# A partial sum scaled by VectorE first and copied by ScalarE, two early rows added up in another order, and narrow unread matmuls in two waits

## The chip, the cores and the metric

The kernel runs on one core of one Trainium2 chip. The metric is the device time of one execution in microseconds (us): the median of a few runs. For the kernel before it is 197.96 us (three runs, 197.57 to 198.35).

A core has five engines that matter here. TensorE (PE in the profile; PEld is its weight load) multiplies matrices into PSUM, an accumulation memory. VectorE (DVE), ScalarE (ACT) and GpSimd (POOL) do element work, and SyncE (SP) issues transfers. Each engine works off its own instruction list in order; between engines there are only waits on semaphores. Sixteen DMA engines move data between the chip's memory and the core.

## The reference

The computation has two steps. The first is a gated recurrence along 5056 tokens, for 4 batches and 256 channels:

```
f = lb + (1 - lb) * sigmoid(f_logit)
h[t] = f[t] * h[t-1] + (1 - f[t]) * x[t]
```

The second is a soft mixture of 8 experts with 4 slots each, on all 4 x 5056 = 20224 rows h:

```
logits = h @ phi                         # 32 slots
d = softmax of logits over all rows      # one column per slot
slot_in = d.T @ h                        # 32 x 256
slot_out[e] = relu(slot_in[e] @ w1[e]) @ w2[e]     # w1: 256 x 1024, w2: 1024 x 256
c = softmax of logits over the 32 slots  # one row per token
out = c @ slot_out                       # 20224 x 256, float32
```

No output row can be written before every row's logits are known and all experts are through: `slot_out` stands between the loads and the results.

## The kernel before

**Loads and recurrence.** The tokens of a batch are cut into groups of 512; a group of one batch is a "unit". For each unit SP loads `f_logit` and `x`, ACT takes the sigmoid, POOL multiplies, PE transposes to channels, DVE runs the recurrence as a scan (L313), and PE transposes back. PE forms the logits (L359), ACT their exponentials (L368), kept for all tokens in `etall` with 4 batches x 32 slots on the 128 partitions, and PE adds each group's part to `slot_ps` (L410). POOL issues the loads of the experts' weights (L137, L147), which turn float32 into bf16 on the way; the last weight is loaded in three pieces, into `w_t`.

**The drain.** After the last unit, PE closes the slot sums (L455). Two waits follow. In the first, DVE copies the sums out (`slot_sb`, L587) before PE can add up the batches (L591). In the second, DVE and ACT scale the result (`sin`, L602 and L603) before PE can start the experts (L621). In each of them PE works off `spin` (L150): six matmuls of 128 columns of weights on 256 columns of data, all of the first expert's weights, whose output nobody reads. A third `spin` of four stands at L724.

**The experts.** Experts 0 to 3 run side by side (L658) into `so4`. Experts 4 to 7 follow one after the other: for each, eight matmuls (L705), each with one eighth of the hidden units (`wide`) and of the weights. They add to `so_ps`, except for the last four of expert 7, which wait for the last pieces of its weights and go to `sb_ps`. `so_ps` also takes `so4` (L719). When `so_ps` is complete it is scaled by `rcs`, one over the sums of exponentials: `part_b` (bf16, ACT, L712) and `part` (float32, DVE, L713). When `sb_ps` is complete, DVE makes `slot_out` = `sb_ps` x `rcs` + `part` (L728).

**Two early rows.** Rows r = 0 and r = 1 of each run of 16 tokens, in batch 3's first 2048 tokens, don't wait for `slot_out`. PE has multiplied their exponentials with expert 7's hidden units ahead of time (`gs`, L680 and L682), so that four matmuls with the last four weight parts (`early_row`, L692) and one with `part_b` (`early_part`, L698) give each row directly, in `early_ps[r]`. ACT scales them (L734) and SP sends them off (L736).

**The order.** It is written out by hand: the program's order is each engine's order. PE runs two `sb_ps` matmuls, `early_row(0, 0, 2)`, both `early_part`, two `sb_ps` matmuls, `early_row(0, 2, 2)`, `early_row(1, 0, 4)`. The framework that places the waits lets two engines that read one PSUM tile do so one after the other, in program order.

**The results.** For each block of tokens PE multiplies `etall` with `slot_out` (L755) or with `slot_bd`, a form of it made by POOL for two batches at once (L738, L811). DVE (L745) and ACT (L749) divide by the row sums and write to SBUF, and SP sends it off. The first block goes off in five pieces (`pieces`, L774; SP issues at L785), the others in large blocks (`couple`, L804, SP at L817; `whole`, L793, SP at L802; `rest`, L819, SP at L834). SP's order is: both early rows, the five pieces, the blocks.

Of the kernel before, what the change touches and what calls it, by code (L numbers as in the profile page):

```python
# [13 lines left out]
ACT = mybir.ActivationFunctionType  # L14
# [4 lines left out]
def kernel(  # L19
# [10 lines left out]
    nc = tc.nc  # L30
    B, S, D = x.shape
    E = moe_w1.shape[0]
    F = moe_w1.shape[2]
    NS = moe_phi.shape[1]
# [97 lines left out]
    w1_sb = [wts.tile([P, DC, F], BF16, name=f"w1_sb{e}") for e in range(E)]  # L132
# [17 lines left out]
    def spin(dst, k, w):  # L150
        for _ in range(k):
            nc.tensor.matmul(dst[:, ds(0, w)], w1_sb[0][:, 0, :P], w1_sb[0][:, 0, :w],
                             start=True, stop=True, skip_group_check=True)

    W_AT = {9: 1, 17: 1, 25: 1, 31: 1, 32: 1, 33: 2, 34: 3, 36: 6}
    w_next = [0]
# [5 lines left out]
    with tc.tile_pool(name="sp2", bufs=3) as sp2, \  # L162
# [9 lines left out]
        slot_bank = pslot.tile([P, 2, D], F32, name="slot_ps")  # L172
# [215 lines left out]
        def row_sums(i):  # L388

            t0, n_r = blocks[i]  # L390
            ew = etall[:, ds(t0, P * n_r)].rearrange("s (p r) -> s p r", r=n_r)
            for r in range(n_r):
                nc.tensor.matmul(sums[:, ds((t0 // P + r) * B, P)], ew[:, :, r], ones,
                                 start=True, stop=True, skip_group_check=True)
            if i == len(blocks) - 1:
                nc.tensor.matmul(rs_ps[:, n_grp * R - 1, ds(0, B // 2)],
                                 left.rearrange("s t u -> s (t u)"), pair_ones,
                                 start=True, stop=True, skip_group_check=True)
# [53 lines left out]
        def late_slots():  # L452
            for r in range(R):
                for b in range(B):
                    nc.tensor.matmul(slot_ps[ds(b * NS, NS), :], ets[last][:, r, b],  # L455
                                     hts[last][:, b, r],
                                     start=False, stop=r == R - 1,
                                     skip_group_check=True)
# [20 lines left out]
        for n in range(n_unit):  # L479
# [14 lines left out]
            else:  # L494
# [40 lines left out]
                if n == n_unit - 2:  # L535
                    tail = psp.tile([P, 2, G], F32, name="tail", tag="sp")
# [44 lines left out]
        late_weights()  # L581
        slots(odd)
        late_slots()
        spin(tail[:, 1], 6, D)
        slot_sb = hpool.tile([P, G, DC], BF16, name="slot_sb", tag="h")
        slot_sb = slot_sb.rearrange("p t o -> p (t o)").bitcast(F32)[:, ds(0, D)]
        nc.vector.tensor_copy(slot_sb, slot_ps)  # L587
# [2 lines left out]
        for o in range(DC):  # L590
            nc.tensor.matmul(sin_ps[:, o], slot_v[:, o], rep[:, 0],  # L591
                             start=True, stop=True, skip_group_check=True)
        spin(slot_bank[:, 1], 6, D)

    with tc.tile_pool(name="ew", bufs=1) as ew, \
         tc.tile_pool(name="pm", bufs=2, space=PSUM) as pm, \
# [17 lines left out]
        for q in range(E // Q):  # L614
            hi = ew.tile([P, F], BF16, name=f"hi{q}")
            for k in range(2):
                hi_ps = (psu.tile([P, H], F32, name="hi_ps", tag="up") if q == 0 else
                         pbig.tile([P, H], F32, name="hi_ps", tag=f"hi_ps{k}"))
                for o in range(DC):
                    for j in range(Q):  # L620
                        nc.tensor.matmul(hi_ps[ds(j * NS, NS)], sin[:, o],  # L621
                                         w1_sb[q * Q + j][:, o, ds(k * H, H)],
                                         start=(o == 0), stop=(o == DC - 1),
                                         skip_group_check=True)
# [6 lines left out]
        rcs = ew.tile([P, 1], F32, name="rcs")  # L631
        for q in range(E // Q):
# [4 lines left out]
            if q == 0:  # L637
# [4 lines left out]
                dst = hid[:, :, :, ds(0, SPE)]  # L642
                dst = bass.AP(tensor=dst.tensor, offset=dst.offset,
                              ap=[list(dst.ap[0]), [Q * NS, FC], [NS + SPE, Q], [1, SPE]])
# [11 lines left out]
        for e in range(Q):  # L656
            for fc in range(FC):
                nc.tensor.matmul(so4_ps[ds(fc % 4 * NS, NS), :], hid[:, fc, e],  # L658
                                 w2_sb[e][:, fc],
                                 start=(e == 0 and fc < 4),  # L660
                                 stop=(e == Q - 1 and fc >= FC - 4),
                                 skip_group_check=True)
# [7 lines left out]
        n_late = FC // 2  # L670
        gs = ew.tile([P, n_late, 2, P], BF16, name="gs")
        hi_v = his[1].rearrange("p (c f) -> p f c", f=FC)
        so_ps = pm.tile([P, D], F32, name="so_ps", tag="pm")
# [3 lines left out]
        for i in range(0, n_late, 2):  # L677
            g_ps = psu.tile([P, 2, 2, P], F32, name="g_ps", tag="up")
            for k in range(2):
                nc.tensor.matmul(g_ps[:, k], hi_v[tail_b, FC - n_late + i + k], ex[tail_b],  # L680
                                 start=True, stop=True, skip_group_check=True)
            nc.scalar.copy(gs[:, ds(i, 2)].rearrange("p k r t -> p (k r t)"),  # L682
                           g_ps.rearrange("p k r t -> p (k r t)"))
        part = ew.tile([P, D], F32, name="part")
        part_b = ew.tile([P, D], BF16, name="part_b")
        e_only = ew.tile([P, 2, P], BF16, name="e_only")
# [3 lines left out]
        early_ps = [psu.tile([P, D], F32, name="early_ps", tag="up") for _ in range(2)]  # L690

        def early_row(r, k, n):  # L692
            for i in range(k, k + n):
                nc.tensor.matmul(early_ps[r], gs[:, i, r], w2_sb[E - 1][:, FC - n_late + i],
                                 start=r == 0 and i == 0, stop=i == n_late - 1,
                                 skip_group_check=True)

        def early_part(r):  # L698
            nc.tensor.matmul(early_ps[r], e_only[:, r], part_b, start=r == 1, stop=False,
                             skip_group_check=True)  # L700

        for j in range(Q):
            for fc in range(FC):
                late = j == Q - 1 and fc >= FC - n_late
                nc.tensor.matmul(sb_ps if late else so_ps,  # L705
                                 wide[:, fc, j].rearrange("p b s -> p (b s)"),
                                 w2_sb[Q + j][:, fc],
                                 start=(j == 0 and fc == 0) or (late and fc == FC - n_late),
                                 stop=j == Q - 1 and fc in (FC - n_late - 1, FC - 1),
                                 skip_group_check=True)  # L710
                if j == Q - 1 and fc == FC - n_late - 1:
                    nc.scalar.activation(part_b, so_ps, ACT.Copy, scale=rcs)  # L712
                    nc.vector.tensor_scalar_mul(part, so_ps, rcs)  # L713
                if j == Q - 1 and fc == FC - 3:
                    early_row(0, 0, 2)
                    early_part(0)
                    early_part(1)
            if j == 0:
                nc.tensor.matmul(so_ps, rep2, so4, start=False, stop=False,  # L719
                                 skip_group_check=True)  # L720
                row_sums(1)
            if j == 1:
                row_sums(2)
                spin(unread, 4, D)  # L724
                q = n_grp * R - 1
                nc.vector.reciprocal(rrow[:, wide_r:q], rs_ps[:, wide_r:q])
                nc.vector.reciprocal(rrow[:, q, ds(0, B // 2)], rs_ps[:, q, ds(0, B // 2)])
        nc.vector.scalar_tensor_tensor(slot_out, sb_ps, rcs, part, ALU.mult, ALU.add)  # L728
        early_row(0, 2, 2)
        early_row(1, 0, 4)  # L730
        early = ew.tile([P, 2, D], F32, name="early")
        to_b = out[ds((B - 1) * S, P * wide_r)].rearrange("(p r) d -> p r d", r=wide_r)
        for r in range(2):
            nc.scalar.activation(early[:, r], early_ps[r], ACT.Copy,  # L734
                                 scale=rrow[:, r, ds(B - 1, 1)])
# [140 lines left out]
```

## Time and profile before

| | |
|---|---|
| median of three runs | 197.96 us (197.57 to 198.35) |
| the profiled execution | 198.21 us |
| its span, first to last instruction | 196.4 us |
| PE busy | 149.9 us (76%), 1196 matmuls |
| DVE busy | 144.1 us (73%) |
| ACT busy | 142.6 us (73%) |
| POOL busy | 103.3 us (53%) |
| read from memory, written to it | 58.23 MB, 20.71 MB |
| chain that ended last | DMA 37%, PE 25%, DVE 13%, ACT 5%, POOL 4%, issue 4% |

No engine is busy all the time, and the chain changes hands often. A share of busy time is a mean over stages with different limits; it has to be read by stage. The profile's page cuts the span into 40 slices for that. The row PEclk there is the share of TensorE's full clock that was granted, in tenths. A chain entry "DMA x" is the time from a transfer's issue to its landing, and "issue" is time in which an engine waited for nothing that the profile shows. In a timeline, the bracket at the end of a line gives the idle time before an instruction and what ended it.

### The profile page before, as it was taken

The numbers are of one execution on the slowest core, as the hardware profiler recorded it, in microseconds if no ns is written. First come the engines' busy times: TensorE is split into PE (matmuls) and PEld (weight loads), VectorE is DVE, ScalarE is ACT, GpSimd is POOL, SyncE is SP. The second block draws the span as 40 slices with busy tenths as digits, with TensorE's granted clock in tenths as the row PEclk, the third lists the DMA queues.
The fourth block names the chain that finished last, engine by engine and source line by source line (L and its number), as shares of the span: only waits on it lengthen the run. The fifth ranks groups of instructions, "written<-read, shape, count | busy, mean of one in ns | idle before, by whom it ended". The sixth has DMA issues, their size and how long they took to land.

```text
span 196.4 us, 3258 instructions
## 1 busy us (share of the span) xinstructions
PE 149.9 (76%) x1196; PEld 105.8 (54%) x1196; DVE 144.1 (73%) x185; ACT 142.6 (73%) x201; POOL 103.3 (53%) x78
## 2 busy tenths in 40 slices
PE   0687579789979979897998888999889999920000
PEld 0475458577766858665776766668664434300000
DVE  2669789998799999999999999343277988920000
ACT  3688778899699998999998797334089999950000
POOL 2689586894988588894969976291030000000000
PEclk9999999996999999999999999999995555555555
DMA  6999999999999999999999999999749999999994
GB/s 205 420 422 418 430 430 420 427 425 333 405 427 424 398 343 422 427 417 308 405 419 385 259 222 214 214 214 213 138 162 432 422 432 424 427 427 437 444 444 173
DMA packets 14161, 70.75 MB, mean 360 GB/s; under 512 B 1585, under 2 KB 2866, under 8 KB 10178
## 3 DMA queue, kind: packets, MB, share of 16 engines
q1 hardware_dynamic: 11520, 62.13, 76.5%
q0 software_dynamic: 2624, 8.42, 21.5%
q8 instruction: 9, 0.15, 0.3%
q14 instruction: 6, 0.05, 0.1%
q10 hardware_dynamic: 2, 0.00, 0.0%
HBM read 58.23 MB, written 20.71 MB: 402 GB/s over the span
## 4 chain that ended last, share of the span: by engine, by line
DMA 37%; PE 25%; DVE 13%; ACT 5%; POOL 4%; issue 4%; ACTq 0%; SPq 0%; POOLq 0%
DMA x_t<-in_x_dram 14%; DVE h L313 10%; PE op L811 8%; DMA w_t<-in_moe_w_dram 8%; DMA f_t<-in_f_logit_dram 7%; DMA w_sb<-in_moe_w_dram 7%; POOL u_t L246 4%; PE hp L326 4%; ACT oc L749 3%; PE up L267 3%; DVE ht L345 3%; PE sp L261 2%; PE op L755 2%; PE lg L359 1%; PE slot_ps L183 1%
## 5 line engine op out<-in xcount | busy, mean ns | idle before, releaser
L246 POOL TENSOR_TENSOR u_t<-s_t,x_t 128x1024 bf16<-128x1024 bf16 (+1 forms) x39 | 82.5, 2131 | 21.8 <-ACT s_t L235 12.3
L313 DVE TENSOR_TENSOR_SCAN h<-a,h,up 128x512 bf16<-128x512 f32 (+1 forms) x72 | 86.9, 1253 | 3.9 <-PE up L267 2.6
L235 ACT ACTIVATE s_t<-f_t 128x2048 bf16<-128x2048 f32 (+2 forms) x23 | 38.4, 1669 | 7.1 <-DMA f_t<-in_f_logit_dram 7.1
L326 PE MATMUL hp<-ident_f,h 128*128 128x128 f32 (+1 forms) x160 | 29.4, 308 | 8.0 <-DVE ht L345 5.8
L326 PEld LDWEIGHTS hp<-ident_f,h 128*128 128x128 f32 (+1 forms) x160 | 23.4, 207 | 18.7 <-DVE ht L345 10.9
L261 PE MATMUL sp<-ident_f,s_t 128*128 128x128 f32 x144 | 21.3, 291 | 6.8 <-ACT s_t L235 4.5
L295 ACT ACTIVATE a<-sp,lbs 128x1024 f32<-128x1024 bf16 x24 | 25.5, 1117 | 0.6 <-PE sp L261 0.6
L749 ACT ACTIVATE oc<-op,rrow 128x256 f32<-128x256 f32 x62 | 24.5, 508 | 0.2
L811 PE MATMUL op<-slot_bd,etall 64*128 64x512 bf16 x62 | 23.6, 594 | 0.4 <-POOL slot_bd L738 0.3
L261 PEld LDWEIGHTS sp<-ident_f,s_t 128*128 128x128 f32 x144 | 17.4, 150 | 8.7 <-ACT s_t L235 5.0
L745 DVE TENSOR_TENSOR oc<-op,rrow 128x512 f32<-128x512 f32 x31 | 20.0, 685 | 2.0 <-PE op L811 1.9
L302 ACT ACTIVATE a<-sp,lbs 128x512 f32<-128x512 bf16 (+2 forms) x22 | 17.8, 857 | 3.8 <-PE sp L261 3.5
L267 PE MATMUL up<-ident_f,u_t 64*128 64x64 f32 x192 | 17.6, 229 | 2.4 <-POOL u_t L246 2.4
L183 PE MATMUL slot_ps<-rep,ident_f 128*128 128x256 f32 x52 | 17.0, 422 | 1.0 <-POOL rep L86 1.0
L267 PEld LDWEIGHTS up<-ident_f,u_t 64*128 64x128 f32 x192 | 13.9, 138 | 6.3 <-POOL u_t L246 2.8
L811 PEld LDWEIGHTS <-etall 64*128 64x128 bf16 x62 | 9.2, 155 | 13.5 <-issue 7.8
L345 DVE COPY ht<-hp 128x512 f32<-128x512 f32 (+1 forms) x20 | 13.4, 670 | 1.4 <-PE hp L326 1.4
L345 ACT COPY ht<-hp 128x512 f32<-128x512 f32 (+1 forms) x20 | 11.7, 583 | 3.5 <-PE hp L326 3.4
L313 DVE TENSOR_TENSOR_SCAN h<-a,up 128x512 bf16<-128x512 f32 x8 | 9.3, 1207 | 2.5 <-PE up L261 2.5
L183 PEld LDWEIGHTS slot_ps<-rep,ident_f 128*128 128x128 f32 x52 | 8.3, 193 | 3.0 <-POOL rep L86 1.2
L359 PE MATMUL lg<-h,phi 128*32 128x512 bf16 (+1 forms) x80 | 9.4, 389 | 0.3 <-ACT et L383 0.2
L261 PE MATMUL up<-ident_f,u_t 128*128 128x128 f32 x48 | 8.9, 314 | 0.5 <-POOL u_t L246 0.5
(126 smaller groups left out, 150.3 us busy)
## 6 DMA issues: line engine op xcount, KB each, us to landing
f_t<-in_f_logit_dram SPq DMA_DIRECT2D x12, 1024.0 KB, 13.3
x_t<-in_x_dram SPq DMA_DIRECT2D x12, 1024.0 KB, 12.0
out_dram<-oc SPq DMA_DIRECT2D x6, 2048.0 KB, 13.7
w_sb<-in_moe_w_dram POOLq DMA_DIRECT2D x14, 512.0 KB, 11.1
f_t<-in_f_logit_dram SPq DMA_DIRECT2D x12, 512.0 KB, 8.4
x_t<-in_x_dram SPq DMA_DIRECT2D x12, 512.0 KB, 9.9
out_dram<-oc SPq DMA_DIRECT2D x4, 896.0 KB, 6.3
out_dram<-ob SPq DMA_DIRECT2D x1, 2048.0 KB, 9.8
```

What stands on the lines that cost most here:

```text
L183: nc.tensor.matmul(slot_bank[:, 1], ident_f, wide_rep, start=False, stop=False, skip_group_check=True)
L235: nc.scalar.activation(s_t, f_t, ACT.Sigmoid, scale=-1.0)
L246: nc.gpsimd.tensor_tensor(uts[n][:, :r], s_t[:, :r], x_t[:, :r], ALU.mult)
L261: nc.tensor.transpose(ps[:, :, r], t[:, r], ident_f)
L267: nc.tensor.transpose(v[:, :, r], t(r)[k].bitcast(F32), ident_f[k, k])
L295: nc.scalar.activation(a, sp[:, :, :, :, o], ACT.Identity, scale=nomlb[:, ds(o, 1)], bias=1.0)
L313: nc.vector.tensor_tensor_scan(h[:, :T, o], decays[n // 2, o][:, n % 2, :T], up[:, :T, o], hs[number(g - 1, b)][:, ds(used(g - 1) - 1, 1), ...
L326: nc.tensor.transpose(hp[:n_p, r], hw[:, :n_p, r], ident_f)
L345: copy(hts[g][:n_p, b].rearrange("p r d -> p (r d)").bitcast(F32), hps.pop(n)[:n_p].rearrange("p r c -> p (r c)"))
L745: nc.vector.tensor_tensor(ob, op, scale.broadcast_to(list(ob.shape)), ALU.mult)
L749: nc.scalar.activation(ob[:, i], op[:, i], ACT.Copy, scale=scale[:, i])
L811: nc.tensor.matmul(op.rearrange("p u d -> p (u d)"), ew[:, :, r], slot_bd[ds(j * 2 * NS, 2 * NS)].rearrange("s u d -> s (u d)"), start=Tru ...
```

## The change

Three edits. The line numbers before L157 stay; later ones move by 6 or 7.

1. `part` comes first, from `so_ps`, by DVE; ACT then makes `part_b` as a plain copy of `part`.
2. The order of PE's matmuls for the two early rows: the first two of both rows stand ahead of the last two `sb_ps` matmuls, and `early_part` closes each row's sum.
3. In the two waits of the drain, `spin` goes from six matmuls to two, and 21 narrow ones follow: 32 columns of the same weights on the same 256 columns of data, with the output going round the four groups of 32 partitions.

```diff
+    def narrow(dst, k):
+        for i in range(k):
+            nc.tensor.matmul(dst[ds(i % B * NS, NS), ds(0, D)], w1_sb[0][:, 0, ds(0, NS)],
+                             w1_sb[0][:, 0, ds(0, D)], start=True, stop=True,
+                             skip_group_check=True)
...
-        spin(tail[:, 1], 6, D)
+        spin(tail[:, 1], 2, D)
+        narrow(tail[:, 1], 21)
...
-        spin(slot_bank[:, 1], 6, D)
+        spin(slot_bank[:, 1], 2, D)
+        narrow(slot_bank[:, 1], 21)
...
         def early_row(r, k, n):
             for i in range(k, k + n):
                 nc.tensor.matmul(early_ps[r], gs[:, i, r], w2_sb[E - 1][:, FC - n_late + i],
-                                 start=r == 0 and i == 0, stop=i == n_late - 1,
-                                 skip_group_check=True)
+                                 start=i == 0, stop=False, skip_group_check=True)
 
         def early_part(r):
-            nc.tensor.matmul(early_ps[r], e_only[:, r], part_b, start=r == 1, stop=False,
+            nc.tensor.matmul(early_ps[r], e_only[:, r], part_b, start=False, stop=True,
                              skip_group_check=True)
...
                 if j == Q - 1 and fc == FC - n_late - 1:
-                    nc.scalar.activation(part_b, so_ps, ACT.Copy, scale=rcs)
                     nc.vector.tensor_scalar_mul(part, so_ps, rcs)
+                    nc.scalar.copy(part_b, part)
                 if j == Q - 1 and fc == FC - 3:
                     early_row(0, 0, 2)
-                    early_part(0)
-                    early_part(1)
+                    early_row(1, 0, 2)
...
         nc.vector.scalar_tensor_tensor(slot_out, sb_ps, rcs, part, ALU.mult, ALU.add)
-        early_row(0, 2, 2)
-        early_row(1, 0, 4)
+        for r in range(2):
+            early_row(r, 2, 2)
+            early_part(r)
```

PE gets 34 matmuls more (42 narrow ones in, 8 wide ones out). DVE, ACT, POOL and SP have the same instructions as before but for `part_b`, a copy with no scale.

## The prediction

> **What bounds the kernel now.** I read the page's 40 slices first: which resource is full where.
>
> ```profile
> PEclk9999999996999999999999999999995555555555
> DMA  6999999999999999999999999999749999999994
> GB/s 205 420 422 418 430 430 420 427 425 333 405 427 424 398 343 422 427 417 308 405 419 385 259 222 214 214 214 213 138 162 432 422 432 424 427 427 437 444 444 173
> ```
>
> A slice is 4.91 us. The DMA engines are full up to about 141 us (loads; 214 GB/s with full engines while weights are converted on the way) and full again from about 146 us to the end (results). Only slices 28 and 29, at 138 and 162 GB/s, are open. The page counts 20.71 MB written, some 48 us at 432 to 444 GB/s. So the end is set by when the writes get going; work before 141 us counts only if it makes the last weight piece late. Next the chain that ended last, in order of time (start, length, what):
>
> ```profile
> 124.82 0.28 issue
> 125.11 16.37 DMA w_t<-in_moe_w_dram
> 141.47 0.04 issue
> 141.52 0.39 PE sb_ps L705 x2
> 141.91 0.22 PE early_ps L694 x2
> 142.13 0.27 PE early_ps L699 x2
> 142.40 0.22 PE sb_ps L705 x2
> 142.62 0.23 PE early_ps L694 x2
> 142.85 0.12 issue
> 142.97 0.49 DVE slot_out L728
> ```
>
> Through both spins of the drain (126.46 and 127.55) the chain is in a transfer: they are not on it. The arithmetic half of the change stands in the 2 us behind that transfer. Last, the timeline there, and SP's queue, which issues all results (columns: start, length):
>
> ```profile
> 141.50 0.47 ACT L712 ACTIVATE part_b<-so_ps,rcs 128x256 bf16<-128x256 f32 x1 [5.84 <-PE so_ps L705]
> 142.01 0.48 DVE L713 TENSOR_SCALAR part<-so_ps,rcs 128x256 f32<-128x256 f32 x1 [2.64 <-ACT part_b L712]
> 142.97 0.48 DVE L728 SCALAR_TENSOR_TENSOR slot_out<-sb_ps,rcs,part 128x256 bf16<-128x256 f32 x1 [0.48 <-PE early_ps L694]
> 143.41 1.67 SPq L736 DMA_DIRECT2D out_dram<-early  x2
> 145.18 2.37 SPq L785 DMA_DIRECT2D out_dram<-ob  x5
> ```
>
> DVE's `part` waited for ACT's `part_b`, though it doesn't read it. And SP goes from one issue to the next: by the line view the two early issues take 0.35 and 1.23 us, the five behind them 0.39 to 0.41 each. The first whole piece (DVE, 143.99 plus 0.69) is ready at 144.68; SP takes it at 145.18.
>
> **The change, part by part.** Times are of the profiled execution: span 196.4, execution 198.21, 0.25 above the median of 197.96 (197.57 to 198.35).
>
> *Narrow matmuls.* Each of two waits loses four wide unread matmuls and gets 21 of 32 columns that go round the four 32-partition groups of the output. The nearest row is L455, the same shape:
>
> ```profile
> 125.91 0.62 PE L455 MATMUL slot_ps<-ht,et 128*32 128x256 bf16 x16
> 126.46 0.83 PE L152 MATMUL tail<-w_sb 128*128 128x256 bf16 x6
> ```
>
> One lasts 0.275 in both. Six wide ones start (0.83 - 0.275) / 5 = 0.11 apart. Sixteen narrow ones in 0.62 are four sets of four, (0.62 - 0.275) / 3 = 0.115 between sets: a set costs as much as one wide matmul. So 21 make six sets. A change of width costs more: the last L455 set starts at 125.91 + 0.62 - 0.275 = 126.25, the first wide one at 126.46, 0.21 instead of 0.11; from L636 to L658 it is 131.56 to 131.72, also 0.10 over the pace there. First wait: two wide (126.46, 126.57), narrow sets from 126.78 to 127.33, L591 at 127.53 instead of 127.12: +0.41. Second: starts 0.41 later, two wide, sets up to 128.81, L621 at 128.82 to 128.92 instead of 128.30 (the change of width that stood before L621 only moves): +0.5 to +0.6 in all. That leaves the path before 141 us. TensorE waits four times before the last piece, counted from start to start less one step: 0.41 at L680 (134.17, for ACT's `ex`), 0.13 at 137.14, 0.70 at 139.56 and 0.37 at 140.80 (all for weights), and 0.28 more at 141.52: 1.9 us. What sets `ex` is POOL's memset of `wide` up to 132.49, which doesn't move; the weight issues on POOL (last at 127.54) wait for earlier transfers, not for TensorE. Cost 0; without that cover +0.6.
>
> The Trainium skill speaks against this part (TensorE: Matmul & The Clock Gate, "Part 3: Packing small matmuls — row/col tiling"): weight loads overlap running matmuls only where the row group differs, and all narrow ones here use all rows. The trace doesn't agree: the L455 rows hold sixteen in 0.62 us. By the rule the time is that of rival D.
>
> *`part` first.* DVE's `part` now waits for TensorE alone. The last matmul into `so_ps` starts at 141.13, its signal let ACT start at 141.50; DVE starts at 141.44 to 141.50 and is done by 141.98 instead of 142.49. ACT's copy starts behind it. A copy of 128x256 f32 from SBUF isn't in the trace; the bounds are 0.47 (L712, the same size from PSUM) and 0.75 (L669, strided), and I take 0.47, the nearer in shape: `part_b` at 142.45, at most 142.75. Before it was 141.97, but now it is needed later.
>
> *The order on TensorE.* Before: sb, sb, early0 x2, part0, part1 (142.02, held by `part_b`), sb, sb (last start 142.35), early0 x2, early1 x4. After: sb, sb, early0 x2, early1 x2, sb, sb, early0 x2, part0, early1 x2, part1. The two part matmuls are swapped for two early ones that wait for nothing, so the last sb matmul starts at 141.52 + 7 x 0.11 = 142.29: -0.06. More isn't to be had: the third sb matmul waits for the last piece of `w_t`, whose signal is complete at 142.10 in the trace, and it would start at 142.18. part0 comes up at 142.62, behind `part_b` by 0.17; with the slow bound it waits 0.13. early0 is then complete one matmul (0.05) later net of the -0.06, early1 likewise, so SP's early issues move from 143.41 to 143.46 (up to 143.6).
>
> *`slot_out`.* It started 0.48 after `part` ended and 0.35 after the modelled end (142.62) of the last sb matmul. If it keeps that 0.35 behind TensorE it gains 0.06. If `part` was what held it, it starts at 142.60 and gains 0.37; other DVE work starts 0.05 behind such an end (L587 at 126.58 against 126.53), so I take -0.37. The 32-row matmuls, the first pieces and POOL's `slot_bd` come forward with it, the first piece to 144.3.
>
> *Where it lands.* SP is the bound there. early1 is issued from 143.91; with the same 1.23 us SP is free at 145.14 and takes the first piece at 145.23, +0.05; the four behind follow 0.49 apart, as before. These five carry 1.75 MB, 4 us at 430 GB/s, so the engines are full from 146 on whether data was ready earlier or not. Is 1.23 us fixed? The issues of L817, L834 and L802 include 1.18, 1.20 and 1.37 us under other conditions; it looks like a property of such an issue, not of what runs beside it. I take it as fixed. Bounds for this part: +0.2 (slow copy) to -0.75 (early1's issue takes 0.35: SP is free at 144.3, as the first piece gets ready).
>
> Sum: 0 (narrow, hidden) + 0.05 (SP) on 198.21, that is 198.26; on the median 198.0.
>
> **The rivals.** About 0.5% (1 us) is what a measurement of this kernel can tell from no change.
> - A, the forecast: SP's second early issue sets the first piece. For it: SP's back-to-back issues. 198.0, with its own range 197.5 to 198.5. Chance 0.52.
> - B: that issue ends earlier along with what runs beside it, and the whole -0.37 comes through. For it: L817's issues vary from 0.33 to 1.20 in one form. 197.6. Chance 0.24.
> - C: the issue shrinks to 0.35 us: -0.75, 197.2. Chance 0.08.
> - D, the other side: narrow matmuls follow each other at 0.11 instead of four at once. Place: both waits. 21 x 0.11 less 4 x 0.11 is 1.87, with the changes of width 2.0 for the first and 1.9 for the second: TensorE 3.9 us late; above 1.9 us it decides. Less that cover +2.0: 200.0. Against it: L455. Chance 0.05.
> - E: the clock. It halved from 44.9 to 48.3 and again at 147.3 (PEclk). If the new mix lets it halve before 141.5, the 11 matmuls from there to early0's end take 0.22 each: early rows and `slot_out` 1.2 us late, 199.2. Against it: slices 26 and 27, full of 32-column matmuls, keep the full clock. Chance 0.05.
> - F: the change does nothing it says: no SP shift and no gain; 198.0, within A's range. Chance 0.06.
>
> **How the numbers follow.** The likeliest is A, 198.0. Leaving D and E out, the range goes from C's 197.2 to 198.8 (A with the slow copy, 0.2, and 0.6 of uncovered drain). Faster by over 0.5% (below 197.0): half of C and a little of B, 0.06. Slower (above 198.95): D, most of E and some drift of A, 0.11. The rest, 0.83, is within 0.5%.
>
> **What would show it.** Right: narrow matmuls in sets of four, 0.11 apart; L591's successor near 127.5; the last weight piece still near 141.5; `part` straight behind `so_ps` and `slot_out` near 142.6; SP's first piece still near 145.2. Wrong: SP's first piece earlier (B, C), TensorE reaching the last piece late (D), PEclk under 9 before slice 29 (E), or `slot_out` still at 142.9.

## The result and the profile after

The kernel after takes 198.74 us (median of 20 executions, 198.01 to 199.07), the kernel before 198.05 beside it (20 executions, 197.57 to 198.40). The ratio is 1.0028, with a 95% interval of 1.0020 to 1.0036: 0.69 us slower. That is under the 0.5% named in the prediction and inside its range, but it is not zero, and the forecast had +0.05.

The profiled execution of after took 198.20 us with a span of 196.4, and that of before 198.21 with 196.4. These two profiles alone would say that nothing changed. First the page's rows for clock and DMA, to be laid beside those of before:

```profile
PEclk9999979999987999999999999999995555555555
DMA  5999999999999999999999999999849999999993
GB/s 195 416 420 420 427 427 424 427 424 351 391 427 424 419 320 427 424 414 342 372 419 422 240 213 214 214 214 214 146 158 433 419 431 424 427 427 444 450 437 170
```

The shape is the same: full engines to about 141 us, two open slices, full engines to the end. The clock is full from 126 to 146 us. The chain that ended last looks different (start, length, what):

```profile
127.48 0.62 PE slot_ps L461 x16
...
128.43 0.76 PE tail L157 x21
129.19 0.59 PE tail L598 x4
...
140.92 1.31 PE so_ps L712 x12
142.23 0.22 PE sb_ps L712 x2
...
143.55 0.48 ACT early L741
144.04 0.04 issue
144.08 1.68 PE op L762 x14
```

Before, this stretch of the chain was one transfer (`w_t`), and the drain was not on it. Now the whole drain with its narrow matmuls is on it, and at 140.92 TensorE goes through all twelve matmuls with no wait for a weight. At the end of the sums ScalarE's first early row stands between TensorE's sums and the first 32-row matmul, where `slot_out` stood before. The timeline of the same kernel:

```profile
128.04 0.39 PE L152 MATMUL tail<-w_sb 128*128 128x256 bf16 x2
128.36 0.83 PE L157 MATMUL tail<-w_sb 128*32 128x256 bf16 x21
129.12 0.66 PE L598 MATMUL tail<-rep,slot_sb 128*128 128x32 f32 x4
...
143.24 0.48 DVE L734 SCALAR_TENSOR_TENSOR slot_out<-sb_ps,rcs,part 128x256 bf16<-128x256 f32 x1 [0.48 <-PE sb_ps L712]
```

The drain starts 1.58 us later than in the profile of before (first wide unread matmul at 128.04, then 126.46), because the recurrence ended later: its last scan starts at 123.36, then 121.78. The kernel's change stands behind that point. Last, SP's queue:

```profile
144.09 0.82 SPq L743 DMA_DIRECT2D out_dram<-early  x2
145.21 2.74 SPq L792 DMA_DIRECT2D out_dram<-ob  x5
```

The two early issues take 0.35 and 0.38 us in place of 0.35 and 1.23. So this execution is late by 0.83 us at the last matmul into `so_ps` (141.96, then 141.13), gets 0.26 back in the sums and 0.60 at SP, and ends where before ended. **The 20 executions of after fall into two groups.** Six, all with a mean granted clock of 0.856, take 198.01 to 198.24, and this profile is one of them. Fourteen, with 0.847 to 0.851 or 0.867 to 0.875, take 198.63 to 199.07, and the median is one of those. By their clocks the fourteen are of two sorts, six at 0.847 to 0.851 and eight at 0.867 to 0.875. The second profile of after (after_again, below) is one of the eight; none of the six was profiled.

One measure makes all profiles comparable. From SP's second whole piece (the second issue of `ob`) to the last result packet it is 48.97 us in before, and 48.93 to 49.00 in 13 of the 14 profiles taken. In these 13, what an edit does up to that issue comes out at the end unchanged.

### The profile page after: what moved, and what is told of

Same layout as the page of the kernel before. It is cut to its first block, busy times and chain, and to the rows that moved or that the text cites. A ratio compares the mean times of both kernels' runs of the same rounds, so it can differ in the third digit from the quotient of the medians.

```text
span 196.4 us, 3325 instructions
## 1 busy us (share of the span) xinstructions
PE 152.8 (78%) x1230; PEld 108.9 (55%) x1230; DVE 144.0 (73%) x185; ACT 142.4 (73%) x201; POOL 103.2 (53%) x78
## 4 chain that ended last, share of the span: by engine, by line
PE 36%; ACT 15%; DVE 15%; DMA 15%; issue 5%; POOL 1%; SPq 0%; ACTq 0%
DMA f_t<-in_f_logit_dram 15%; DVE h L319 12%; PE op L818 9%; ACT s_t L241 4%; PE hp L332 4%; PE sp L267 4%; ACT a L308 3%; ACT oc L756 3%; DVE ht L351 3%; PE up L273 3%; PE op L762 3%; ACT a L301 2%; PE so_ps L712 2%; PE slot_ps L189 1%; PE lg L365 1%
## 5 line engine op out<-in xcount | busy, mean ns | idle before, releaser
L267 PE MATMUL sp<-ident_f,s_t 128*128 128x128 f32 x144 | 22.2, 300 | 6.3 <-ACT s_t L241 4.6
L267 PEld LDWEIGHTS sp<-ident_f,s_t 128*128 128x128 f32 x144 | 18.2, 155 | 8.2 <-ACT s_t L241 5.4
L273 PE MATMUL up<-ident_f,u_t 64*128 64x64 f32 x192 | 17.9, 231 | 2.0 <-POOL u_t L252 1.8
L189 PE MATMUL slot_ps<-rep,ident_f 128*128 128x256 f32 x52 | 17.5, 433 | 0.2 <-POOL rep L86 0.2
L267 PE MATMUL up<-ident_f,u_t 128*128 128x128 f32 x48 | 9.8, 338 | 0.5 <-POOL u_t L252 0.5
```

The lines of the kernel that those rows point to most:

```text
L189: nc.tensor.matmul(slot_bank[:, 1], ident_f, wide_rep, start=False, stop=False, skip_group_check=True)
L267: nc.tensor.transpose(ps[:, :, r], t[:, r], ident_f)
L273: nc.tensor.transpose(v[:, :, r], t(r)[k].bitcast(F32), ident_f[k, k])
```

## The experiments

Each run stands beside runs of the kernel before on the same chip: medians 198.07 (29 executions), 198.04 (29) and 198.10 (17) for the three batches.

Five theories were set against each other, by the numbers that the expectations use. 1: the longer drain costs, because where the recurrence ends late TensorE has no wait left to hide it. 2: the other order of the sums costs, because the first 32-row matmul waits for ScalarE's first early row. 3: the narrow form itself costs, or lowers the clock. 4: TensorE's instruction fetch, a transfer of its own, holds what runs beside it, and its shift decides. 5: SP's long issue belongs to its place, the second early transfer.

### Batch 1: each half alone, and the length of the drain

**narrow_only**: before, with the two waits of after and nothing else.

```diff
-        spin(tail[:, 1], 6, D)
+        spin(tail[:, 1], 2, D)
+        narrow(tail[:, 1], 21)
...
-        spin(slot_bank[:, 1], 6, D)
+        spin(slot_bank[:, 1], 2, D)
+        narrow(slot_bank[:, 1], 21)
```

> The two waits of the drain have two wide and 21 narrow matmuls as in the changed kernel; the sums are as before. Theory 1 (the longer drain: in the changed profile TensorE comes to the last weight piece without a wait, and the two waits take 0.4 and 0.1 us longer): this edit alone costs what the change costs, 198.05 to about 198.6, and TensorE shows no wait for w_t. Theory 2 (the other order of the sums: the first 32-row matmul now waits for ScalarE's first early row, 0.3 us after slot_out): this edit costs nothing, 198.0. Theory 3 (the clock): slower, with PEclk falling at other places than in the kernel with ten and eight wide matmuls.

Measured: 199.00, ratio 1.0046 (1.0028 to 1.0064). The loss sits in this edit. **arith_only**: after, with the waits of before.

```diff
-        spin(tail[:, 1], 2, D)
-        narrow(tail[:, 1], 21)
+        spin(tail[:, 1], 6, D)
...
-        spin(slot_bank[:, 1], 2, D)
-        narrow(slot_bank[:, 1], 21)
+        spin(slot_bank[:, 1], 6, D)
```

> Six wide matmuls in both waits as before, but the sums in the changed order. Theory 1: 197.8 to 198.1, as before or 0.2 us faster, since slot_out's start moves from 1.56 to 1.0 us behind the end of so_ps while the first 32-row matmul moves from 2.1 to 1.8. Theory 2: all of the loss, about 198.6. Theory 3: 198.0.

Measured: 198.15, ratio 1.0008 (0.9996 to 1.0021). The other order of the sums costs nothing that shows; theory 2 falls as the cause of the loss.

**wide_10_8**: before, with a drain as long as that of after, made of wide matmuls.

```diff
-        spin(tail[:, 1], 6, D)
+        spin(tail[:, 1], 10, D)
...
-        spin(slot_bank[:, 1], 6, D)
+        spin(slot_bank[:, 1], 8, D)
```

> The kernel before with ten and eight wide matmuls in the two waits, about as long as the two wide and 21 narrow ones (1.08 and 0.87 us). Theory 1: the same time as the narrow kernel, about 198.6, since only the length counts. Theory 2: 198.0. Theory 3 (the narrow form moves the clock): 198.0, away from the narrow kernel.

Measured: 198.42, ratio 1.0013 (0.9995 to 1.0031). The drain, from the copy to `slot_sb` to the first expert matmul, is 2.34 us, as in after (2.33; before 1.72). Its profile has the cover that the prediction counted on: the recurrence ends at 121.89, and the first `sb_ps` matmul starts at 141.57 (before: 141.52). The interval reaches from -0.1 to +0.6 us, so this run neither clears the length alone nor shows that it costs.

**short_2_2**: before, with two wide matmuls in each wait (`spin(..., 2, D)`), a drain of 1.55 us.

```diff
-        spin(tail[:, 1], 6, D)
+        spin(tail[:, 1], 2, D)
...
-        spin(slot_bank[:, 1], 6, D)
+        spin(slot_bank[:, 1], 2, D)
```

> The kernel before with two wide matmuls in each wait, the sums as before; TensorE idles the rest of the waits. Theory 1: TensorE leaves the drain 0.1 us earlier or none (the waits then end with the copy and with sin), so 197.8 to 198.0. Theory 2: 198.0. Theory 3 (the unread matmuls hold the clock): slower than before, over 198.5, with PEclk under 9 somewhere between 126 and 145 us.

Measured: 198.70, ratio 1.0033 (1.0016 to 1.0049). A shorter drain is slower too, so its length can't be the whole story. Its profile is of one of its slower executions (199.27). There the second whole piece is issued 1.07 us later than in before: 0.61 of that stand ahead of the first 32-row matmul (144.12 against 143.51), behind a recurrence that ended late (last scan at 123.85), and 0.46 at SP:

```profile
144.01 0.87 SPq L736 DMA_DIRECT2D out_dram<-early  x2
145.31 3.30 SPq L785 DMA_DIRECT2D out_dram<-ob  x5
```

The early issues are short here (0.35 and 0.43), and the first whole piece has the long one: 1.33 of the 3.30 us. The long issue is not tied to the second early row (theory 5 falls). It moved by one place when eight matmuls went away.

What did move with it is a transfer that no edit names: TensorE's instruction fetch. The page of after lists it (packets, MB, share of 16 engines' span):

```profile
q8 instruction: 9, 0.15, 0.3%
```

That is 16 KB each. From the first fetch of after to the last, 2061 of TensorE's instructions start in eight steps, 258 a step, so a packet holds about that many. Its packets' times in the trace, beside SP's long issue:

| | fetch begins, us | takes | ends | SP's long issue ends |
|---|---|---|---|---|
| before | 143.74 | 0.96 | 144.70 | 145.09 (second early row) |
| before_again | 143.26 | 1.03 | 144.29 | 144.66 (second early row) |
| arith_only | 143.48 | 1.12 | 144.60 | 145.02 (second early row) |
| wide_10_8 | 143.81 | 1.00 | 144.81 | 145.23 (second early row) |
| short_2_2 | 145.07 | 1.19 | 146.26 | 146.64 (first whole piece) |
| after_pad94 | 144.55 | 1.36 | 145.91 | 146.29 (second early row) |
| after | 141.67 | 0.98 | 142.65 | none |
| narrow_only | 141.51 | 0.95 | 142.46 | none |

In these six profiles the held issue ends 0.37 to 0.42 us behind the fetch; every other issue of the early rows and the first whole piece takes 0.33 to 0.46, in all 14 profiles. To lie beside the fetch is not enough, though: in before_again the first early issue lies inside it (143.46 to 143.80) and takes 0.35. Nor does a long issue need the fetch: in before six of SP's later issues (L817, L834, L802) take 1.18 to 1.37 us with no fetch beside them, and it is alike in the other profiles. That the fetch holds SP rests on these six cases and on the long issue moving and vanishing with it; how it does so is not shown. The 42 narrow matmuls for 8 wide ones are 68 instructions more (a load and a matmul each), and the fetch came 2.1 us earlier in after than in before.

### Batch 2: the instructions without the drain

The next kernels add matmuls of two columns, unread, at the very start (behind `enter(0)`, before the first loads have landed). They lengthen neither wait of the drain and shift TensorE's instruction stream by as much as the narrow matmuls do.

**before_pad** and **arith_pad**: before, and arith_only, each with 34.

```diff
         enter(0)
+        for _ in range(34):
+            nc.tensor.matmul(slot_bank[:, 1, ds(0, 2)], ident, ident[:, ds(0, 2)],
+                             start=True, stop=True, skip_group_check=True)
```

> The kernel before with 34 matmuls of two columns added at the very start, where TensorE waits for the first load; their output is not read. They shift TensorE's instruction list by 68, as the narrow matmuls do, and make no wait longer. Theory 4 (TensorE's instruction fetch, 16 KB at 143.7 us in the profile before, holds SP's issue beside it for 0.85 us; the narrow matmuls move that fetch to 141.5): the long issue is gone, SP takes the first piece when it is ready, 1.15 us behind the first 32-row matmul, 144.7 instead of 145.2: 197.5. Theory 5 (the long issue belongs to the second early transfer or to the place in SP's list): as before, 198.05, with an issue of over 1 us near 144.

Measured: 198.53, ratio 1.0028 (1.0017 to 1.0038).

> The changed sums, six wide matmuls in both waits, and the 34 matmuls at the start. Theory 4: the long issue is gone, and the earlier first 32-row matmul (by 0.1 to 0.3 us) comes through: 197.3. Theory 5: as the sums alone, 198.1. If the 34 matmuls slow the start or move the clock, both padded kernels show it before 30 us.

Measured: 198.76, ratio 1.0034 (1.0016 to 1.0053), 0.61 us above arith_only; its 12 executions spread from 197.56 to 199.81, more than any other kernel's. Neither theory gave these times: SP's early issues are short in both (0.35 and 0.38 to 0.39), and both kernels are slower. By count alone, with the drain of before, 34 matmuls cost about what after costs. Four transfers write `w_t`, the whole weight of expert 6 and then the three pieces of expert 7's; they are counted in that order here. In arith_pad the fetch begins at 140.42, and the third and fourth land at 142.60 and 143.07 instead of 141.48 and 142.11; TensorE waits for them. Its chain (start, length, what):

```profile
125.01 17.59 DMA w_t<-in_moe_w_dram
142.60 0.05 issue
```

Fifteen of the 16 DMA engines had signalled the third transfer by 141.41; only the sixteenth came at 142.60. The profile of before_pad is its slowest execution (199.25). Its fetch begins at 141.82, the whole weight stream is 0.77 later than in before, and the fourth transfer lands at 143.95, 1.72 behind the third, where it is 0.63 in before; again fifteen engines are through by 142.85. Why the whole stream is late there is open. The late recurrence (123.91) alone doesn't do it: that of narrow_only ends at 123.85, and its weights land within 0.06 us of before's.

**arith_pad_bank**: arith_pad, with the early rows' sums in banks of PSUM that the first `op` tiles don't share.

```diff
-        early_ps = [psu.tile([P, D], F32, name="early_ps", tag="up") for _ in range(2)]
+        early_ps = [pbig.tile([P, H], F32, name="early_ps", tag=f"hi_ps{1 - i}")[:, :D]
+                    for i in range(2)]
```

> As the kernel with the changed sums and the 34 matmuls, but the early rows' sums lie in two other PSUM banks, so that the first 32-row matmul waits for slot_out alone and not for ScalarE's first early row. Theory 4: the first 32-row matmul starts 0.05 behind slot_out instead of 0.36, and up to 0.3 us come off: 197.0. Theory 5: 198.1, since SP's long issue sets the first piece.

Measured: 198.59, ratio 1.0029 (1.0016 to 1.0041), within the noise of arith_pad. In the profile the edit does what it should: the first 32-row matmul starts 0.06 behind `slot_out` and 1.81 behind the last `so_ps` matmul, where after has 2.12. What that is worth in the time did not show; its weights are 0.35 late as well (third transfer at 141.83).

**after_pad94**: after with 94 such matmuls, to bring the fetch round to its old place by SP's issue.

> The changed kernel with 94 matmuls of two columns at the start: with the narrow ones' 68 instructions that is a shift of 256, one whole fetch, so that a fetch falls where it fell before the change. Theory 4: an issue of SP near 144 to 145.5 takes over 1 us again, in a kernel whose data is already late: 198.8 to 199.4. Theory 5: as the changed kernel, 198.7, with no long issue.

Measured: 199.43, ratio 1.0078 (1.0058 to 1.0098). The fetch lies at 144.55 and SP's second early issue is long again, 1.29 us: that part came as expected. But all transfers into `w_t` are late too (the third 142.56, the fourth 143.16). It is again one engine of 16: fifteen have signalled the first by 139.69, the sixteenth comes at 140.61, and in the other three it is 0.92 to 0.98 behind. The fetch before that lies at 136.12, and it fits as the cause; but in short_2_2 a fetch at 136.99 makes no engine late, so that stays open.

### Batch 3: the fetch put where it meets nothing

**after_n8**: after with 8 narrow matmuls in each wait instead of 21: 16 instructions more than before, in place of 68.

```diff
-        narrow(tail[:, 1], 21)
+        narrow(tail[:, 1], 8)
...
-        narrow(slot_bank[:, 1], 21)
+        narrow(slot_bank[:, 1], 8)
```

> The changed kernel with 8 narrow matmuls instead of 21 behind the two wide ones in each wait: the narrow form and its changes of width stay, but two sets of four take the place of six, so the waits are about as short as with six wide matmuls. Theory 1 (the length of the drain costs): 198.0 to 198.2, as the changed sums alone; from the last scan to the last matmul into so_ps 18.0 to 18.2 us where the recurrence ends late, not 18.6. Theory 3 (the narrow form itself): 198.6 or more.

Measured: 197.59 (12 executions, 197.38 to 197.95), ratio 0.9982 (0.9972 to 0.9992): 1.15 us under after, and the only kernel of the study that beats before. Both theories had 198.0 or more, so neither gives this time. The fetch runs from 142.47 to 143.71, behind the third and the fourth transfer into `w_t` (141.46 and 142.09) and ahead of SP's second early issue (143.91); the first, from 143.46, takes 0.35. The chain and SP's queue:

```profile
125.11 16.36 DMA w_t<-in_moe_w_dram
141.46 0.05 issue
141.51 0.39 PE sb_ps L712 x2
...
142.92 0.48 ACT early L741
143.41 0.04 issue
143.45 1.68 PE op L762 x14
```

```profile
143.46 0.82 SPq L743 DMA_DIRECT2D out_dram<-early  x2
144.58 2.62 SPq L792 DMA_DIRECT2D out_dram<-ob  x5
```

The weights are on time and the early issues are short. **before_again** and **after_again**: the two kernels unchanged, profiled once more, to see how much a profile differs from another of the same kernel.

> The kernel before, profiled once more, to see where its recurrence ends in another execution. Theory 1: if the last scan starts at 123 us or later, the last matmul into so_ps follows by 18.0 us and TensorE hardly waits for w_t; if it starts near 121.8, by 19.3, because TensorE waits for w_t. The end is the second piece's issue plus 49.0 us either way.

Measured: 197.81, span 196.0. The same wait for weights as in the first profile of before (third transfer 141.47 in both); the long issue is 0.76 instead of 1.23, since the fetch began 0.48 earlier.

> The changed kernel, profiled once more. Theory 1: 18.6 us from the last scan to the last matmul into so_ps if the recurrence ends late; if it ends near 121.8, TensorE waits for w_t again and the last matmul into so_ps starts near 141.2. No issue of SP over 1 us between 143 and 148. The end is the second piece's issue plus 49.0 us.

Measured: 198.92, span 197.0, mean clock 0.869: an execution of the larger group. The recurrence ends as early as in before (last scan at 121.87), so the drain has its cover again: the last matmul into `so_ps` starts at 141.06, no later than in before (141.13). Chain and SP's queue:

```profile
125.04 17.62 DMA w_t<-in_moe_w_dram
142.66 0.05 issue
142.71 0.39 PE sb_ps L712 x2
...
144.12 0.48 ACT early L741
144.60 0.04 issue
144.65 1.68 PE op L762 x14
```

```profile
144.66 0.82 SPq L743 DMA_DIRECT2D out_dram<-early  x2
145.78 2.70 SPq L792 DMA_DIRECT2D out_dram<-ob  x5
```

Line by line it is after_n8 shifted by 1.20 us, and the shift is there from the first line on: the transfer takes 17.62 instead of 16.36. The fetch began at 140.58 and took 0.98. In the trace, 15 of the 16 DMA engines had signalled the third transfer by 141.36, as in before and after_n8 (15 by 141.32, the sixteenth 0.15 later); here the sixteenth came at 142.66. One engine was late, by somewhat more than the fetch took. In after and narrow_only the fetch begins at 141.67 and 141.51, when the last weight packets are going through, and no engine is late. arith_pad_bank is an exception that stays open: its fetch begins at 141.51 too, its fourth transfer lands at 142.46, and the fetch makes no engine later.

**best_pad90**: arith_only with the banks of arith_pad_bank and 90 matmuls of two columns at the start, to place the fetch ahead of the last weights.

> The changed sums with the early rows in two other PSUM banks, six wide matmuls in the waits, and 90 matmuls of two columns at the start: a shift of 180 instructions, so that one instruction fetch of TensorE falls near 138 and the next near 150, none between 139 and 148. Theory 4 (a fetch beside SP's issues, or beside the last weight piece, costs up to 0.9 us): no issue of SP over 1 us before 150, the last weight piece lands near 142.1, SP takes the first piece when it is ready: 197.2 to 197.8, ahead of both kernels. If the fetch is worth nothing in the end: 198.0.

Measured: 199.25, ratio 1.0062 (1.0049 to 1.0075): a miss. The weights did not come as expected: the fourth transfer lands at 142.88, not near 142.1, with one engine 0.8 behind the others in all four and a fetch at 136.46. No fetch lies beside SP's first issues, and the second whole piece goes at 145.66, as in before. But the next fetch begins at 155.43, among the results, and the last result packet comes 50.12 behind that piece instead of 48.97. It is the one profile of 14 that leaves that figure. The landings show the same pattern as the weights: of the result issued at 149.77 the sixteenth engine is 0.31 behind the other fifteen, of the next one (151.78, landing past the fetch) 1.61, and it is still 0.94 behind in the last that can be read. That the fetch is what held this engine is inferred from its place.

## Why the prediction was right and where it was wrong

**Where the difference comes from.** From after_again to before_again, second whole piece 146.20 against 145.23, +0.97: weights 142.71 against 141.52 at the first `sb_ps` matmul, +1.19; from there to the first 32-row matmul 1.94 against 2.04, -0.10; from there to the piece 1.55 against 1.67, -0.12. Against the first profile of before, with its longer issue (2.15), it is +1.19 - 0.05 - 0.60 = +0.54. The medians differ by 0.69.

The forecast was 198.0 and the kernel takes 198.74, inside the range only because the range reached to 198.8 for an uncovered drain and a slow copy. In after_again the drain is covered and the copy is fast, and another term makes the loss. As far as that profile speaks for the median, it is luck that the time lies inside the range.

**Narrow matmuls: the step that failed.** Their size was right. Sets of four follow each other at about 0.11 us (21 in 0.83), and L598 starts 1.08 behind the first wide matmul, forecast 1.07. The Trainium skill's rule on weight loads (TensorE: Matmul & The Clock Gate, "Part 3: Packing small matmuls — row/col tiling"), weighed in the prediction as rival D, is contradicted again by these 0.83 us; the drain is 0.61 longer (2.33 against 1.72), forecast 0.5 to 0.6. What failed is "Cost 0", in two ways:

- *The cover was that of one execution.* In executions where the recurrence ends early, TensorE waits for weights and the 0.61 vanish, as forecast (after_again). In the profiles of after, narrow_only, short_2_2 and arith_pad_bank it ends at 123.4 to 124.3, and TensorE meets no wait for `w_t`: last scan to last `so_ps` matmul is 18.6 in the first two and 17.9 in the others, arith_pad_bank with the drain of before among them. There the 0.6 ("without that cover +0.6") is paid. wide_10_8, the same length with only 12 instructions more, is at +0.35 with an interval from -0.1 to +0.6, so what this is worth in the median isn't shown.
- *The instructions themselves were not counted.* 68 more on TensorE move its fetch from beside SP's issue (143.3 to 143.7) to 140.6 in after_again, into the last 1.5 us of the weight stream. One of 16 engines delivers its share 1.2 us late, and TensorE waits for it. arith_pad pays the same without a longer drain (+0.61 over arith_only, one engine 1.2 us late), and after_n8, with 16 instructions more, doesn't pay. (Its drain is 1.61 us, so it has neither cost; arith_pad is the run that has the second alone.)

The prediction looked for the cost of a longer wait and priced no transfer, since the diff has none. That all eight executions with a clock like after_again's have this collision is inferred from one profile; what makes the six at 0.847 to 0.851 slow is not shown.

**"Is 1.23 us fixed? ... I take it as fixed": wrong.** It goes with the fetch beside SP's second early issue. The later issues that the prediction took as its evidence stay long in every profile, for a reason that no run here shows. In after the long early issue is gone (0.38), as in rival C, though for another reason than a property of the issue. It gives 0.60 us in the profile of after against that of before, and hides most of the loss above. after_n8 is what rival C would have looked like alone: second whole piece 145.01 against 145.66 in before, -0.65, where C had -0.75; in the medians -0.51. (The five pieces of the first block are 1.84 MB, 4.3 us at 430 GB/s, not 1.75 and 4; nothing hangs on it.)

**`part` first: right.** `part_b` took 0.40, forecast 0.47 with bounds to 0.75. **The order on TensorE: right in size**, 0.05 to 0.10 where weights bind. **`slot_out`, -0.37: right, and worth little.** In after_n8 it starts at 142.60, the forecast instant, against 142.97 before:

```profile
142.60 0.48 DVE L734 SCALAR_TENSOR_TENSOR slot_out<-sb_ps,rcs,part 128x256 bf16<-128x256 f32 x1 [0.69 <-PE sb_ps L712]
```

`part`'s end had held it in before, where it starts 0.48 behind that; in after_n8 it starts 0.69 behind `part` and 0.05 behind the end of the last `sb_ps` matmul. (In the first profile of after it is 0.48 behind `part` again, since there the weights are early against the sums.) But the first 32-row matmul came only 0.06 earlier (143.45 against 143.51). It now waits for ScalarE to read the first early row: `slot_out` is done at 143.08, ScalarE's row ends at 143.40. The first `op` tile and that row share a bank of PSUM; with other banks (arith_pad_bank) the wait is gone. The prediction asked what holds SP next, but not what holds this matmul.

**Rivals and signs.** D and E, and with them theory 3, are refuted: sets of four, PEclk full from 126 to 146 us, and after_n8, which has the narrow form and is faster than before. Of the signs that the prediction named, "last weight piece still near 141.5" holds in after (141.45) and fails in after_again (142.66); "SP's first piece still near 145.2" holds in after (145.21) for the wrong reason, a later start and a shorter issue, and fails in after_again (145.78). F is refuted by `slot_out` in after_n8. **The end is set by SP's pieces and the full engines behind them: right**, 48.97 behind the second one.

**Open.** How often an execution ends its recurrence late. The traces hint at the clock: in the six profiles with 6.8 us or more at half clock in the first 62 us the last scan starts at 123.00 to 124.34, in the eight with 3.4 us or none at 121.76 to 122.89, and after's faster group has one clock (0.856), that of its profile, which has two stretches of 3.4 us; no run tests it. Further: which DMA engine carries the fetch; why the fetch holds some of SP's issues until 0.4 us behind its end and not others; why all weights were late in before_pad, arith_pad_bank, after_pad94 and best_pad90.

## What to carry to other kernels

Count the instructions that an edit adds, not only their time: here each 258 or so on TensorE were a 16 KB transfer of their own, and its place beside the last load or the first result was worth 0.4 to 1.2 us. Before a cost is written off as hidden, see whether the cover is there in a second execution; here the wait that hid 0.6 us was absent in some. And when one wait is shortened, name the next reader of the same PSUM bank: 0.37 us at `slot_out` became 0.06.

## What the runs showed of the hardware

- TensorE's instruction fetch takes 0.9 to 1.4 us here and costs TensorE itself nothing that the trace shows: beside no fetch of the 14 profiles does TensorE idle for over 0.15 us without another wait that ends it. Where it ran within the last 1.5 us of the weights (after_again, arith_pad, before_pad), one engine's signal of 16 came 1.1 to 1.2 us late (in arith_pad_bank none did); past the fetch among the results (best_pad90) one engine was 1.61 behind, 0.31 before it. In six profiles one issue of SP beside the fetch took 0.76 to 1.33 us instead of 0.33 to 0.46. The Trainium skill (Runtime: NRT & Kernel Launch, "Instruction fetch mechanics") has the fetch in 16 KiB blocks of 256 instructions on a DMA queue of its own, mostly hidden. The trace agrees on the blocks (9 packets, 0.15 MB, 258 instructions a step); hidden it is here for the engine that fetches, and not for the transfers beside it.
- Two executions of one kernel can differ by 1.5 us at the end of the recurrence (last scan at 123.36 in after, 121.87 in after_again) and still end 0.6 us apart in the other direction (spans of 196.4 and 197.0).
